# Convolution and routed feed-forward: ids turned later, turns pinned behind results, rows listed for scatter sooner

## The chip, the cores and the metric

The kernel runs on one core of one Trainium2 chip. The metric is the device time of one execution in microseconds. Before the change the median of three runs is 1252.04 us (1251.1 to 1256.04). The engines are named as in the profile: PE is TensorE's matmul, PEld its weight load, DVE is VectorE, ACT is ScalarE, POOL is GpSimd, SP is SyncE, which here only issues transfers.

## The reference, cut to what matters

```
# 1. a causal convolution, 7 taps, 8 heads with their own softmaxed weights
w   = softmax(weight)                       # 8 x 7
x1  = sum over k of w[h, k] * x_pad[b, s + k, h, :]        # x: 8 x 3584 x 192
# 2. each of the 28672 rows goes to one of 8 experts
logits = x1 @ w_gate + modality_bias[modality_id]          # 192 -> 8
e      = argmax(logits);  gate = softmax(logits)[e]
out    = gate * (relu(x1 @ w1[e]) @ w2[e])  # 192 -> 1024 -> 192, in float32
```

## The kernel before, in words

**Routing.** The sequence is cut into blocks of 120 rows. 19 groups of 4, 8 or 16 tiles (`QUADS_OF_GROUP`, in quads of 4 tiles) pass through the same parts (`body`, lines 671 to 705, and `finish`, 655 to 669). A group is convolved on PE into PSUM, one product for a head or a pair of heads, and ACT (some heads: DVE) copies the result into a row buffer `y` (lines 427 to 462; L446, L448 and L460, L462). `turn` (L478) transposes 32 x 32 squares of y on DVE, a quad at a time, so that PE can multiply them by the gate weights (L496, L512). DVE turns the logits back (L503, L518), adds the bias `bt` of the row's modality (L504, L520; POOL makes it at L473 and L476), and `choose` finds the expert. `place` counts the rows of each expert with products of the one-hot choice and keeps a running `carry`; from these come the row numbers `idx` (L620) in a scratch table of routed rows. Groups from 6 on are `tiled`: all 128 partitions are used for the small arrays, and `move` and `take` bring the numbers back into place. `send` lists one scatter a tile: POOL writes 120 rows of y to their places in the scratch table (L347, an indirect DMA).

There are four y buffers, and a group of 16 tiles takes two. So the copies of group g overwrite rows that group g - 2 scatters.

**Experts.** When a chunk of groups has been routed (`GROUPS_OF_CHUNK`), `table` works out on DVE which experts have enough rows for a slot of fixed size. A slot loads its expert's weights (SP, L895 to L900), splits them and its rows into a high and a low part (L110, L112, L980, L982), and runs in steps. A step is 20 products of the first layer (`first`, L995), the relu on ACT (hh, L998), its low part on DVE (hl, L999), and 16 products of the second layer for the step two before (`second`, L1015, L1019). Every four steps `put` weighs the result (lowp on ACT, o on DVE, L1033) and POOL writes two tiles of out (L1037). There are 456 steps.

**Order.** `run` writes steps and routing parts into each other: after each step it advances the routing generator until the parts reach `due(step)`. The first four groups and 59 parts more come before step 0. Scatters and out writes aren't issued where they are written but put into the list `waiting` (`in_turn`); out writes go to its front. After each step `release` takes one out of it, or two when more than `MANY` wait, and makes it wait for the hl of that step (`behind_step`). Before group g is convolved, `release_rows_of(g - 2)` empties the list of that group's rows at once. How fast scatters are listed is set in `all_groups`: the ends of group g - 1 (its place, numbers and scatters: 22 of them) are spread over the parts of group g (25 or 29). ACT's instructions within the steps keep the order in which they are written. The other engines' lists are ordered by a planner, which takes what it holds to be ready; `tc.issue_after(ins)` puts what is inside it behind `ins` on the same engine and adds nothing else. `turn_squares`, the transposes of a slot's rows, are already behind `state["o"]`, which is the last hl or o that has been written.

**Modality ids.** Those of groups 0 to 5 come first, by POOL's DMAs. Those of the later groups are loaded by SP (`load_later`, L307) into the second weight buffer `raw1[1]`, and `make_mods`, called in front of group 5, casts them (L252), transposes them (L254), and hands them to all later `bias_of`. `make_tiled` (L229) builds the tables of the tiled groups on POOL; its last two operations (L245, L246) are DVE's.

Of the kernel before, what the change touches and what calls it, by code (L numbers as in the profile page):

```python
# [9 lines left out]
F32 = mybir.dt.float32  # L10
# [4 lines left out]
ALU = mybir.AluOpType  # L15
AX = mybir.AxisListType
PSUM = bass.MemoryType.PSUM

P = 128
MB = 120  # L20
# [16 lines left out]
AHEAD = 59  # L37
SPLIT = 46
T = 256
MANY = 4  # L40
GROUPS_OF_CHUNK = (4, 3, 2, 2, 2, 2, 2, 2, 0, 0)
SLOTS_OF_CHUNK = (3, 2, 3, 4, 3, 4, 4, 3, 4)
PASSES_OF_SLOT = (2, 4, 4, 4, 4, 4, 4, 4, 2, 1)
# [8 lines left out]
def conv_then_routed_ffn(ctx, tc, x, weight, modality, w_gate, mod_bias, w1, w2, out):  # L52
    nc = tc.nc
    NB, S, D = x.shape
    H, K = weight.shape
    E, _, FF = w1.shape
# [9 lines left out]
    OVER = 2  # L66
    Q = 32
    NK = D // Q
    W = D + OVER
# [9 lines left out]
    const = ctx.enter_context(tc.tile_pool(name="const", bufs=1))  # L79
# [11 lines left out]
    turns, state = {}, {}  # L91

    def ring(pool, n, shape, dtype, name, tag=None):

        tag = tag or name
        k = turns[tag] = turns.get(tag, -1) + 1
        return pool.tile(shape, dtype, name=name, tag=f"{tag}_{k % n}", bufs=1)
# [10 lines left out]
    def split(hi, lo, raw, behind=None):  # L108
        with tc.issue_after(behind[0]) if behind else nullcontext():
            nc.scalar.copy(out=hi, in_=raw)  # L110
        with tc.issue_after(behind[1]) if behind else nullcontext():
            return nc.vector.tensor_tensor(out=lo, in0=raw, in1=f(hi), op=ALU.subtract).ins  # L112


    def make_marks():
# [27 lines left out]
                      in_=weight.rearrange("h k -> (h k)").partition_broadcast(K * DIAG))  # L143
# [12 lines left out]
    def warm(n):  # L156
# [9 lines left out]
        out=tri, in_=ones, compare_op=ALU.is_gt, fill=0.0, base=0,  # L166
# [62 lines left out]
    def make_tiled():  # L229

        wide = const.tile([P, NK, Q], F32, name="wg_wide")
        nc.gpsimd.memset(wide, 0.0)
        same = const.tile([P, P // Q, Q], F32, name="same")
        part = const.tile([P, P // Q], F32, name="part")
        nc.gpsimd.memset(part, 0.0)
        for q in range(P // Q):
            rows = slice(q * Q, (q + 1) * Q)
            nc.gpsimd.memset(part[rows, q:q + 1], 1.0)
            nc.gpsimd.tensor_copy(out=wide[rows, :, q * E:(q + 1) * E], in_=wg[rows])
            nc.gpsimd.tensor_copy(out=same[rows], in_=ident[rows, rows].unsqueeze(1).broadcast_to([Q, P // Q, Q]))  # L240
        ramps = const.tile([P, P // Q, E], F32, name="ramps")
        nc.gpsimd.iota(ramps, pattern=[[0, P // Q], [-1, E]], base=E, channel_multiplier=0,
                       allow_small_or_imprecise_dtypes=True)
        real = const.tile([P, 1], F32, name="real")
        nc.vector.tensor_reduce(out=real, in_=same[:, 0, 0:MB % Q], axis=AX.X, op=ALU.add)  # L245
        nc.vector.tensor_scalar(out=ramps[:, MB // Q, :], in0=ramps[:, MB // Q, :], scalar1=real, scalar2=None, op0=ALU.mult)  # L246
        return wide, same, part, ramps

    def make_mods():

        low = raw1[1][:, 1, 0:LOTS * P].rearrange("p (b s) -> p b s", s=Q)
        nc.vector.tensor_copy(out=low, in_=later.rearrange("p l (q s two) -> p (l q) s two", s=Q, two=2)[:, :, ::-1, 0])  # L252
        mods = const.tile([P, LOTS, P // Q, Q], F32, name="mods")
        nc.vector.transpose(out=mods.rearrange("p l q r -> p (l q r)"), in_=low.rearrange("p b s -> p (b s)"))  # L254
        return mods
# [44 lines left out]
    def load_later():  # L300
        nc.vector.memset(later[:, LOTS - 1, :].bitcast(F32), 0.0)
        for c in range(P // Q):
            for lot in range(LOTS):
                n = min(8, NG - TILED - 8 * lot)
                b, sb = c % 2 * 4, EARLY + 16 * lot + c // 2
                at = 2 * (b * S + sb * MB - CUT + MB - P)
                nc.sync.dma_start(out=later[c * Q:c * Q + 4 * n, lot], in_=bass.AP(words.tensor, words.offset + at, [  # L307
                    [4 * MB, n], [2 * S, 4], [1, 2 * P]]))
# [4 lines left out]
    later = raw1[1][:, 0, 0:LOTS * 2 * P].bitcast(I32).rearrange("p (l w) -> p l w", l=LOTS)  # L313
# [15 lines left out]
    def release(n=1):  # L329
        while waiting and n:  # L330
            op, _ = waiting.pop(0)
            n -= op() is not None
# [36 lines left out]
    class Group:  # L369
# [108 lines left out]
        def turn(self, q):  # L478

            t0 = self.b0 + 4 * q % NB  # L480
            if not self.tiled:
                dst = ring(gp, 2, [P, NK, 4, Q], F32, "turned")
                self.quad_turned.append(dst)
            else:
                if q == 0:
                    self.turned = xp.tile([P, NK, NT, Q], F32, name="gx", tag=self.place_x)
                dst = self.turned[:, :, 4 * q:4 * q + 4]
            nc.vector.transpose(out=dst.rearrange("p k t c -> p t k c"),
                                in_=self.ys[4 * q // NB][:, t0:t0 + 4, OVER:W].rearrange("p t (k c) -> p t k c", c=Q))

        def gate_tiled(self):

# [154 lines left out]
    def parts_of(g):  # L647

        return H + 5 + 3 * QUADS_OF_GROUP[g] + (QUADS_OF_GROUP[g + 1] if WHOLE_X <= g + 1 < NG else 0)

    def ends_of(g):

        return 4 * QUADS_OF_GROUP[g] + (6 if g >= TILED else 1)

    def finish(gr, at_once):
        gr.place()
        yield
        if gr.tiled:
            yield
            yield  # L660
            gr.move()
            yield
            yield
            gr.take()
            yield
        for t in range(0, gr.tiles, at_once):
            gr.send(t, t + at_once)
            yield
        in_turn(lambda: state.update(groups=state["groups"] + 1), gr.g)
# [37 lines left out]
    early, wide = [], []  # L707

    def load_early(g):
        early.append(Group(g, chunk_of[g]))  # L710
        for q in range(early[-1].quads):
            early[-1].load(q)

    def all_groups():

        for g in range(CLEARED, sum(len(p) for p in PACKS)):
            load_early(g)
        with tc.issue_after(state["x"]):
            ins = nc.sync.dma_start(out=scr[DUMMY:DUMMY + TW, :].rearrange("(j p) w -> p j w", p=P),
                                    in_=filler.unsqueeze(1).broadcast_to([P, TW // P, W])).ins  # L720
        tc.add_to_no_dep_group("rows0", ins)
        scatters.append((0, ins.name))
        load_later()
        cur, ends = early[0], iter(())
        for g in range(NG):
            if g == TILED - 1:
                wide.append(make_mods())
            if g == WHOLE_X - 2:
                split(band_hi, band_lo, band)
            after = (early[g + 1:g + 2] or [Group(g + 1, chunk_of[g + 1])])[0] if g + 1 < NG else None  # L730
            done = 0
            for i, _ in enumerate(body(cur, after)):
                yield
                if g < FIRST:
                    if 1 <= i < H:
                        next(ends, None)
                        if i == H - 1:
                            for _ in ends:
                                pass
                elif g == KEPT:  # L740
                    next(ends, None)
                else:
                    while done * (parts_of(g) - 4) < ends_of(g - 1) * i:
                        next(ends, None)
                        done += 1
            for _ in ends:
                pass
            ends = finish(cur, 4 if g < FIRST else 1)
            if g + 1 in (FIRST, NG):
                for _ in range(WAIT):  # L750
                    yield
                for _ in ends:
                    yield
            cur = after
# [291 lines left out]
    plan, tokens, slots, g = [], 0, 0, 0  # L1046
# [18 lines left out]
    start_row, step, low = make_modality()  # L1065
# [5 lines left out]
    with tc.issue_after(state["low"]):  # L1071
        filler = make_filler()
    state.update(carry=carry, groups=0, placed=0, brought=0, parts=0)
    work = all_groups()

    def advance():
        next(work, None)
        state["parts"] += 1
# [18 lines left out]
    for c in range(1, last):  # L1097
        steps += plan[c - 1][1] * steps_of(c - 1)
        g = sum(GROUPS_OF_CHUNK[:c + 1])
# [47 lines left out]
    def run(i0, i1):  # L1147

        lagging, count = [], 0
        for i in range(i0, i1):  # L1150
# [3 lines left out]
            for step in range(steps):  # L1154
# [10 lines left out]
                while i0 == 0 and state["parts"] < due(count):  # L1165
                    advance()
                release(1 + (len(waiting) > MANY))
                if chunk < last and state["placed"] >= sum(GROUPS_OF_CHUNK[:chunk + 2]) and \
# [85 lines left out]
```

## Time and profile before

| | |
|---|---|
| median of the runs | 1252.04 us |
| the profiled execution | 1254.28 us |
| its span, first to last instruction | 1252.2 us |
| mean granted TensorE clock | 0.986 |
| PE busy | 1204.0 us, 96% |
| DVE busy | 930.4 us, 74% |
| ACT busy | 693.2 us, 55% |
| POOL busy | 514.7 us, 41% |

The span is one profiled execution; what a run takes outside it is the 2.1 us between the second and the third line. An engine's busy time is a sum over the whole span; where the engine waits, and for whom, is in the timelines and in the view of waits. An idle time stands in brackets behind an instruction, with the instruction that released it.

### The profile page before, as it was taken

The numbers are of one execution on the slowest core, as the hardware profiler recorded it, in microseconds if no ns is written. First come the engines' busy times: TensorE is split into PE (matmuls) and PEld (weight loads), VectorE is DVE, ScalarE is ACT, GpSimd is POOL, SyncE is SP. The second block draws the span as 40 slices with busy tenths as digits, with TensorE's granted clock in tenths as the row PEclk, the third lists the DMA queues.
The fourth block names the chain that finished last, engine by engine and source line by source line (L and its number), as shares of the span: only waits on it lengthen the run. The fifth ranks groups of instructions, "written<-read, shape, count | busy, mean of one in ns | idle before, by whom it ended". The sixth has DMA issues, their size and how long they took to land. (4 is left out here: it accounts for less than half of the span.)

```text
span 1252.2 us, 28508 instructions
## 1 busy us (share of the span) xinstructions
PE 1204.0 (96%) x9507; PEld 1180.0 (94%) x9507; DVE 930.4 (74%) x2427; ACT 693.2 (55%) x1545; POOL 514.7 (41%) x568
## 2 busy tenths in 40 slices
PE   7889999999999999999999999999999999999996
PEld 6789999999999899998999999999999999999995
DVE  5787887677777777777776786876866766787894
ACT  2365555554655455555555555655555555566783
POOL 6746645534435245262624525335243222222121
PEclk8899999999999999999999999999999999999998
DMA  6787645335534353343543525433254343944271
GB/s 165 215 212 216 138 116 137 82 98 149 142 58 127 83 125 97 67 116 89 150 89 73 123 59 130 101 63 75 76 120 89 83 92 87 274 101 109 43 187 42
DMA packets 307587, 143.85 MB, mean 115 GB/s; under 512 B 221899, under 2 KB 294103, under 8 KB 307430
## 3 DMA queue, kind: packets, MB, share of 16 engines
q1 hardware_dynamic: 283894, 97.57, 35.5%
q0 software_dynamic: 22560, 44.34, 11.3%
q8 instruction: 76, 1.25, 0.4%
q14 instruction: 81, 0.66, 0.2%
q10 hardware_dynamic: 976, 0.03, 0.0%
HBM read 116.13 MB, written 51.81 MB: 134 GB/s over the span
## 5 line engine op out<-in xcount | busy, mean ns | idle before, releaser
L1015 PE MATMUL po<-w2b,hh 128*128 128x384 f32 x1824 | 558.6, 357 | 3.9 <-DVE o L1033 3.9
L995 PE MATMUL hps<-sxh,w1b 128*128 128x256 f32 x1824 | 485.1, 288 | 16.4 <-DVE hl L999 14.8
L999 DVE SCALAR_TENSOR_TENSOR hl<-hps,hh 128x512 fp32r<-128x512 f32 x456 | 313.2, 688 | 217.1 <-ACT hh L998 213.0
L1037 POOL DMA_INDIRECT out_dram<-o,tags x228 | 231.1, 1013 | 554.7 <-DVE o L1033 334.8
L998 ACT ACTIVATE hh<-hps 128x512 fp32r<-128x512 f32 x456 | 273.0, 599 | 320.8 <-PE hps L995 317.1
L1019 PE MATMUL po<-w2b,hl 128*128 128x192 f32 x1824 | 444.2, 254 | 0.0
L995 PEld LDWEIGHTS hps<-sxh,w1b 128*128 128x128 f32 x1824 | 344.6, 189 | 27.8 <-DVE hl L999 24.7
L995 PE MATMUL hps<-sxs,w1b 128*128 128x256 f32 x1824 | 363.4, 281 | 0.3 <-DVE sxs L982 0.2
L1015 PEld LDWEIGHTS po<-w2b,hh 128*128 128x128 f32 x1824 | 345.0, 189 | 5.4 <-DVE o L1033 5.1
L1019 PEld LDWEIGHTS po<-w2b,hl 128*128 128x128 f32 x1824 | 347.5, 191 | 0.0
L347 POOL DMA_INDIRECT routed_rows<-y,idx x240 | 252.4, 1052 | 166.5 <-DVE hl L999 74.2
L995 PEld LDWEIGHTS hps<-sxs,w1b 128*128 128x128 f32 x1824 | 279.7, 189 | 0.7 <-DVE sxs L982 0.4
L995 PE MATMUL hps<-sxl,w1b 128*128 128x256 f32 x912 | 256.7, 282 | 0.7 <-DVE sxl L982 0.7
L995 PEld LDWEIGHTS hps<-sxl,w1b 128*128 128x128 f32 x912 | 173.1, 190 | 0.9 <-DVE sxl L982 0.9
L112 DVE TENSOR_TENSOR w1b<-raw,w1b 128x512 fp32r<-128x512 f32 x152 | 101.7, 678 | 25.1 <-ACT w1b L110 24.9
L1031 ACT ACTIVATE lowp<-po,tags 128x192 f32<-128x192 f32 x228 | 83.8, 419 | 30.9 <-PE po L1015 30.9
L112 DVE TENSOR_TENSOR w2b<-raw,w2b 128x384 fp32r<-128x384 f32 x152 | 80.9, 542 | 19.9 <-ACT w2b L110 19.6
L110 ACT CAST w1b<-raw 128x512 fp32r<-128x512 f32 x152 | 92.8, 621 | 1.9 <-DMA raw<-in_moe_w_dram 0.7
L1033 DVE SCALAR_TENSOR_TENSOR o<-po,tags,lowp 128x192 f32<-128x192 f32 x228 | 84.8, 411 | 2.2 <-ACT lowp L1031 2.2
L980 ACT CAST sxs<-tp 64x128 fp32r<-64x128 f32 x224 | 66.7, 298 | 31.5 <-DVE tp L954 28.8
L110 ACT CAST w2b<-raw 128x384 fp32r<-128x384 f32 x152 | 76.0, 512 | 1.4
L982 DVE TENSOR_TENSOR sxs<-tp,sxs 64x128 fp32r<-64x128 f32 x224 | 64.3, 287 | 9.1
(191 smaller groups left out, 846.8 us busy)
## 6 DMA issues: line engine op xcount, KB each, us to landing
raw<-in_moe_w_dram SPq DMA_DIRECT2D x38, 768.0 KB
raw<-in_moe_w_dram SPq DMA_DIRECT2D x38, 512.0 KB
raw<-in_moe_w_dram SPq DMA_DIRECT2D x76, 256.0 KB
near<-routed_rows SPq DMA_DIRECT2D x208, 64.0 KB
xr<-in_x_dram SPq DMA_DIRECT2D x32, 384.0 KB
x<-in_x_dram SPq DMA_DIRECT2D x26, 384.0 KB
routed_rows<-filler SPq DMA_DIRECT2D x9, 776.0 KB
far<-routed_rows SPq DMA_DIRECT2D x208, 32.0 KB
```

The lines of the kernel that those rows point to most:

```text
L110: nc.scalar.copy(out=hi, in_=raw)
L112: return nc.vector.tensor_tensor(out=lo, in0=raw, in1=f(hi), op=ALU.subtract).ins
L347: state["scatter"] = nc.gpsimd.indirect_dma_start(out=scr, out_offset=bass.IndirectOffsetOnAxis(ap=idx, axis=0), in_=src, in_offset=None,).ins
L980: nc.scalar.copy(out=hi, in_=raw)
L995: nc.tensor.matmul(hps[:, u, :], wa[:, c, fs], mv[z], start=n == 0, stop=n == len(terms) - 1)
L998: state["hh"] = nc.scalar.activation(out=hh, in_=hps, func=AF.Relu).ins
L999: hl_ins = nc.vector.scalar_tensor_tensor(out=hl, in0=hps, scalar=0.0, in1=f(hh), op0=ALU.max, op1=ALU.subtract)
L1015: nc.tensor.matmul(po, hh[:, u, js], wb[:, c, :], start=c == 0, stop=c == NF - 1, skip_group_check=True)
L1019: nc.tensor.matmul(po[:, 0:D], hl[:, u, js], wb[:, c, 0:D], start=False, stop=False, skip_group_check=True)
L1031: nc.scalar.activation(out=lowp, in_=po[:, D:2 * D], func=AF.Copy, scale=gate)
L1033: turn_behind(nc.vector.scalar_tensor_tensor(out=o, in0=po[:, 0:D], scalar=gate, in1=lowp, op0=ALU.mult, op1=ALU.add))
L1037: st = nc.gpsimd.indirect_dma_start(out=out, out_offset=bass.IndirectOffsetOnAxis(ap=at, axis=0), in_=o, in_offset=None, bounds_check=N - ...
```

## The change

Four edits. `MANY` falls from 4 to 3, so two are released after a step when more than three wait. `make_tiled` no longer ends with the two operations on `real` and `ramps`; they move into `make_mods`, and both they and the cast of the later ids (with the transpose that needs it) go behind `state["idx"]`, which at that place of the text is the row numbers of group 3. The transposes of `turn` go behind the last hl or o, as soon as there has been one. And the ends of a group are spread over nine parts fewer than the next group has, where it was four fewer.

```
-MANY = 4
+MANY = 3
...
+        return wide, same, part, ramps
+
+    def make_mods():
+
+        _, same, _, ramps = wide
         real = const.tile([P, 1], F32, name="real")
-        nc.vector.tensor_reduce(out=real, in_=same[:, 0, 0:MB % Q], axis=AX.X, op=ALU.add)
+        with tc.issue_after(state["idx"]):
+            nc.vector.tensor_reduce(out=real, in_=same[:, 0, 0:MB % Q], axis=AX.X, op=ALU.add)
         nc.vector.tensor_scalar(out=ramps[:, MB // Q, :], in0=ramps[:, MB // Q, :], scalar1=real, scalar2=None, op0=ALU.mult)
-        return wide, same, part, ramps
-
-    def make_mods():
-
         low = raw1[1][:, 1, 0:LOTS * P].rearrange("p (b s) -> p b s", s=Q)
-        nc.vector.tensor_copy(out=low, in_=later.rearrange("p l (q s two) -> p (l q) s two", s=Q, two=2)[:, :, ::-1, 0])
+        with tc.issue_after(state["idx"]):
+            nc.vector.tensor_copy(out=low, in_=later.rearrange("p l (q s two) -> p (l q) s two", s=Q, two=2)[:, :, ::-1, 0])
...
-            nc.vector.transpose(out=dst.rearrange("p k t c -> p t k c"),
-                                in_=self.ys[4 * q // NB][:, t0:t0 + 4, OVER:W].rearrange("p t (k c) -> p t k c", c=Q))
+            with tc.issue_after(state["o"]) if "o" in state else nullcontext():
+                nc.vector.transpose(out=dst.rearrange("p k t c -> p t k c"),
+                                    in_=self.ys[4 * q // NB][:, t0:t0 + 4, OVER:W].rearrange("p t (k c) -> p t k c", c=Q))
...
-                    while done * (parts_of(g) - 4) < ends_of(g - 1) * i:
+                    while done * (parts_of(g) - 9) < ends_of(g - 1) * i:
```

## Rows read from the trace of the kernel before

**Rows 1.** The page's first part: busy us, share of the span, instructions.
```profile
PE 1204.0 (96%) x9507; PEld 1180.0 (94%) x9507; DVE 930.4 (74%) x2427; ACT 693.2 (55%) x1545; POOL 514.7 (41%) x568
```

**Rows 2.** Windows: length, busy us of each engine, granted clock, DMA share, GB/s.
```profile
250.00:275.00 25.00, 22.72 (x158) 22.17 (x157) 18.16 (x51) 14.22 (x34) 10.66 (x10) 0.93 0.48 120
...
400.00:425.00 25.00, 21.95 (x156) 21.32 (x156) 17.68 (x39) 14.02 (x31) 9.30 (x9) 0.93 0.71 163
...
550.00:575.00 25.00, 22.85 (x160) 22.29 (x158) 18.03 (x52) 14.04 (x33) 11.01 (x10) 0.93 0.48 123
...
950.00:975.00 25.00, 25.00 (x196) 25.00 (x196) 17.17 (x42) 14.76 (x32) 7.50 (x8) 1.00 0.33 60
```

**Rows 3.** Waits of PE, whole span: total us, times, longest us.
```profile
PE hps L995 <- DVE hl L999: 14.8, 14, 3.0
PE gt L512 <- DVE turned L488: 5.6, 1, 5.6
PE po L1015 <- DVE o L1033: 3.9, 5, 1.7
```

**Rows 4.** Waits of ACT, whole span, in front of the copy into y.
```profile
ACT y L446 <- DMA out_dram<-o,tags: 25.2, 6, 5.2
```

**Rows 5.** Timeline of ACT, 262 to 276: start, us, instruction, idle before.
```profile
266.48 0.77 ACT L446 COPY y<-cv 120x192 f32<-120x192 f32 x3 [4.76 <-DMA out_dram<-o,tags]
```

**Rows 6.** Timeline of POOL, 225 to 300: the last scatter before that copy.
```profile
261.33 0.99 POOL L347 DMA_INDIRECT routed_rows<-y,idx  x1 [0.35 <-DVE hl L999]
```

**Rows 7.** Waits of PE in 250:300, 325:360, 400:430, 550:600, 625:665 and 700:750.
```profile
PE hps L995 <- DVE hl L999: 3.2, 3, 2.3
...
PE hps L995 <- DVE hl L999: 1.6, 1, 1.6
...
PE hps L995 <- DVE hl L999: 3.0, 1, 3.0
...
PE hps L995 <- DVE hl L999: 3.0, 3, 2.1
...
PE hps L995 <- DVE hl L999: 1.9, 1, 1.9
...
PE hps L995 <- DVE hl L999: 1.0, 2, 0.8
```

**Rows 8.** Timeline of DVE: turns before the steps, and in them.
```profile
56.52 3.55 DVE L488 STREAM_TRANSPOSE gx<-y 128x768 f32<-128x768 f32 x4
...
287.63 0.96 DVE L488 STREAM_TRANSPOSE gx<-y 128x768 f32<-128x768 f32 x1
288.53 0.64 DVE L999 SCALAR_TENSOR_TENSOR hl<-hps,hh 128x512 fp32r<-128x512 f32 x1
```

**Rows 9.** Timeline of DVE in the head: the later ids, the tiled logits.
```profile
18.16 0.31 DVE L252 CAST raw<-raw 128x256 f32<-128x256 int32 x1 [6.21 <-DMA raw<-in_moe_modality_id_dram]
...
62.08 0.29 DVE L504 TENSOR_TENSOR lg<-lt,bt 128x128 f32<-128x128 f32 x1
```

**Rows 10.** Timeline of PE in the head: convolution, gate, first step.
```profile
11.65 2.27 PE L457 MATMUL cv<-x,band 128*120 128x96 f32 x18
19.50 2.90 PE L512 MATMUL gt<-turned,wg_whole 128*128 128x128 f32 x12 [5.58 <-DVE turned L488]
...
62.67 0.51 PE L995 MATMUL hps<-sxh,w1b 128*128 128x256 f32 x2
```

**Rows 11.** Timeline of POOL in the head: tables, bias, scatters.
```profile
19.10 0.18 POOL L242 IOTA ramps<- 128x32 f32 x1
20.02 0.83 POOL L473 TENSOR_TENSOR bt<-mods,step 128x128 f32<-128x128 f32 x2 [0.74 <-DVE mods L254]
...
27.96 1.11 POOL L347 DMA_INDIRECT routed_rows<-y,idx  x1 [6.28 <-DVE oh L557]
...
53.34 1.12 POOL L347 DMA_INDIRECT routed_rows<-y,idx  x1 [0.30 <-issue]
...
57.76 0.99 POOL L347 DMA_INDIRECT routed_rows<-y,idx  x1 [0.30 <-issue]
```

More of the change, by code (lines that the diff above doesn't have):

```diff
@@ L243, in make_tiled @@
                        allow_small_or_imprecise_dtypes=True)
-        real = const.tile([P, 1], F32, name="real")
-        nc.vector.tensor_reduce(out=real, in_=same[:, 0, 0:MB % Q], axis=AX.X, op=ALU.add)
-        nc.vector.tensor_scalar(out=ramps[:, MB // Q, :], in0=ramps[:, MB // Q, :], scalar1=real, scalar2=None, op0=ALU.mult)
         return wide, same, part, ramps
     def make_mods():
+        _, same, _, ramps = wide
+        real = const.tile([P, 1], F32, name="real")
+        with tc.issue_after(state["idx"]):
+            nc.vector.tensor_reduce(out=real, in_=same[:, 0, 0:MB % Q], axis=AX.X, op=ALU.add)
+        nc.vector.tensor_scalar(out=ramps[:, MB // Q, :], in0=ramps[:, MB // Q, :], scalar1=real, scalar2=None, op0=ALU.mult)
         low = raw1[1][:, 1, 0:LOTS * P].rearrange("p (b s) -> p b s", s=Q)
-        nc.vector.tensor_copy(out=low, in_=later.rearrange("p l (q s two) -> p (l q) s two", s=Q, two=2)[:, :, ::-1, 0])
+        with tc.issue_after(state["idx"]):
+            nc.vector.tensor_copy(out=low, in_=later.rearrange("p l (q s two) -> p (l q) s two", s=Q, two=2)[:, :, ::-1, 0])
         mods = const.tile([P, LOTS, P // Q, Q], F32, name="mods")
```

## The prediction

> **What bounds the kernel now.** I read the windows first, then the waits, then the timelines around the waits. TensorE (PE) is busy 1204.0 of 1252.2 us [rows 1], and in the late stretch 950 to 975 it is busy for all of it at full clock [rows 2]. So a step costs what PE needs for it, and this change touches no matmul. What can move is the 48 us in which PE stands, and the clock that is lost behind a pause: in the stretches at 250, 400 and 550 PE is busy 21.95 to 22.85 of 25 us and the granted clock averages 0.93, so it has fallen to its lower level, 1.2 GHz, for part of them [rows 2]. At 0.93 for 25 us, 0.07 x 25 = 1.75 us of full-speed work is lost in each.
>
> The waits of PE sort into three kinds. Most is PE waiting for hl, 14.8 us in 14 waits, then 5.6 us in one wait for a turned row, then 3.9 us for o [rows 3].
>
> First kind: y that can't be overwritten. ACT copies the convolution into y, and ACT runs in written order, so what stands behind that copy (the relu hh of a step) stands too. These copies waited 25.2 us in six waits [rows 4]; the one at 266.48 waited 4.76 us for a DMA [rows 5]. The last scatter from the rows that it overwrites was issued at 261.33 and off POOL at 262.32 [rows 6], so it took 4.2 us more to land. The view names a write of out as the releaser; no operand of the copy has to do with out, and a wait for several signals is put down to the one that came last, so I read it as the scatter. PE then waits for hl: longest waits 2.3, 1.6, 3.0, 2.1, 1.9 and 0.8 us, one for each of the six copies, 11.7 us [rows 7].
>
> Second kind: turns of a group in a bunch. At 287.63 DVE runs a turn of 0.96 us, and hl starts right behind it at 288.53 [rows 8]. The third and fourth turn of that group are written several steps apart, but DVE's list has them in a row. What is left of PE's waits for hl, 14.8 - 11.7 = 3.1 us, and the 3.9 us for o are of this kind: 7.0 us.
>
> Third kind: the head. DVE's copy of the later modality ids stands 6.21 us for its DMA until 18.16 [rows 9], and the first turned rows stand behind it. PE, done with two groups' convolutions at 13.92, waits 5.58 us for them until 19.50 [rows 10].
>
> **The change part by part.**
>
> Rows five parts sooner, and MANY 3. No instruction is added: the same 240 scatters, listed and released earlier. I counted through the rules of `release`, `release_rows_of` and `ends` step by step. Before, 3 to 5 scatters of a group are still waiting when the group two later starts, and are all released in the step that also issues that group's convolution (groups 7 to 16). After, none of them is: the last one is released 5 or 6 steps ahead for groups 9 to 16 and 2 steps ahead for groups 7 and 8; group 6 stays as it is (8 left in place of 9). From 62.67 [rows 10] to the end 456 steps take 2.6 us each, so five steps are 13 us, against 4.2 us to land. The six waits should go, and with them three of the clock dips: 11.7 + 3 x 1.75 = 16.9 us. What is late next there is DVE: the row-number chain of the group before starts in the same steps. I take 14 of the 16.9 us; bounds 0 (landing is set by something else) and 16.9. Two releases a step from a queue of four fill POOL earlier, not more; POOL is busy for 514.7 of 1252.2 us [rows 1], so it costs nothing while the out writes stay in front, which `in_turn` sees to.
>
> Turned rows behind a step's results. 13 groups have four turns each; 12 of them (48 turns of 0.96 us) are issued within the steps. Pinned behind the last hl or o, no turn can be drawn forward, and the bunches fall apart into one turn in two to four steps. Gain at most 7.0 us, all waits of the second kind. Queued behind a pinned turn on DVE are the other splits and transposes of that step; who waits for the turn itself is the gate product on PE. The choice of an expert is written 5 to 8 steps behind the last turn, and the row numbers come after that, so a turn that is 0.96 us late has room. Below nothing: PE runs in order, and if a gate product is put too early in its list, PE stands for the turn; the nearest rows are 5.58 us in the head [rows 10] and, per group, one step of 2.6 us. I take 3.5 us gained, half of the upper bound, since the turns of the first group in the steps are written in successive steps and stay dense.
>
> Modality ids behind the first row numbers. Removed from in front of the first turn: the copy with its 6.21 us, and the transpose and the two small operations on `real` and `ramps`, all moved behind the fourth group's row numbers, where they cost DVE at most 4 x 0.31 [rows 9], about 1 us. DVE was free for the first turn at 18.16 - 6.21 = 11.95; the gate product behind that turn then stands behind the convolutions, at 13.92 in place of 19.50, and at full clock, since the stretch without PE work goes. From there to the first scatter the rows take 27.96 - 19.50 = 8.5 us [rows 10, 11], part of it at the lower clock. POOL is the floor: its preparation of the tiled tables ends at 19.10 + 0.18 [rows 11], so the first scatter can't be much ahead of 19.7: at most 8.2 us sooner than 27.96. From there POOL paces the head: 20 scatters (4, 4, 8 and 4 tiles of the first four groups) start from 27.96 to 53.34 [rows 11], and the first slot's rows are read when the 20th has landed. The two bias pairs on POOL (`bt`, 0.83 us for the first two operations [rows 11], about 1.7 us for all four) need the ids and move from in front of the scatters to among them; they delay the scatters behind them by 1.7 us, or not the first slot's at all if they come behind the 20th. The ids lie in the weights' second buffer, which is asked for only after the first slot's rows are. I take 6 us sooner for the first step; bounds 8.2 us, and 1 us later (DVE's moved 1 us with nothing won). PE is the bound of all that follows, so the lead stays to the end.
>
> A rule of the skill against it: the scatter at 57.76 took 0.99 us under four turns that ran on DVE from 56.52 on, 3.55 us long [rows 8, 11], as long as others. The Trainium skill, SBUF — State Buffer, section "SBUF: two separate sides", says that while a VectorE operation holds the port pair that it shares with GpSimd, GpSimd can't write the descriptors of its DMAs until that operation ends. The pin makes turn and scatter start together, both being released by hl. By the rule a scatter would land up to 0.96 us later, which hurts only groups 7 and 8 with their two steps: 1.9 us more of ACT's waits, of which PE lost 11.7 / 25.2, so 0.9 us, and the sum would be 1230. By the row it costs nothing, and I go by the row.
>
> **Sum.** 14 + 3.5 + 6 = 23.5 us. The profiled execution took 1254.28 us, 2.1 outside its span; less 23.5 that is 1230.8. The median of the runs shown is 1252.04, and from that it is 1228.5. I say 1229.
>
> **Rivals.**
>
> A. The head's lead is lost (0.20). If POOL's list has the bias pairs behind all 32 early scatters (20 take 25.4 us [rows 11] and 12 more another 16, with what lies between 43), they run at 19.7 + 43 = about 63, and the logits of the first tiled group, at 62.08 before [rows 9], come no sooner; if the first step's operations stand behind them, the head gains nothing. For it: POOL is full then. Against it: nothing makes step 0 need them. Time: 1252 - 17.5 = 1234.5.
>
> B. Listing sooner doesn't free y (0.13). The landing of 4.2 us [rows 5, 6] may be set by the loads of the next slot's rows, which fill the DMA engines then, or the wait may be for the out write that is named. Then the six waits stay, and only head and turns change; with both at half, 1252 - 5 = 1247. Against it: 13 us is far more than 4.2.
>
> C. Slower (0.09): PE stands for late turns. One mechanism: the gate products sit in PE's list where the planner thinks the last turn ends; on the chip hl is late, the turn behind it too, and PE stands up to one step, 2.6 us, in each of 12 groups: 31 us, against 20 us won in the two other parts (14 + 6): 1252 + 11 = 1263. It decides from 20 / 12 = 1.7 us a group. For it: PE has already waited 5.58 us for one turn. Against it: a group's turns have steps of room before anything needs them.
>
> **How the numbers follow.** Forecast 0.58, A 0.20, B 0.13, C 0.09. The forecast's own range is 1219 (everything at its upper bound, 16.9 + 7.0 + 8.2 = 32.1 less) to 1240. With A inside and part of B, the range is 1218 to 1250. A measurement of this kernel tells apart about 0.5%, 6 us. Forecast and A are faster by more; B is within it: faster 0.78, same 0.13, slower 0.09.
>
> **What would show it.** ACT's waits for a DMA in front of L446 gone (25.2 us before), PE's waits for hl under 6 us, the windows that had 0.93 at 1.00. No two turns (L488) in a row on DVE after the first step. First scatter near 20, first product L995 near 56. I am wrong if PE's idle time in the steps moves to another wait, above all `gt` for `gx`, or if the first scatter is early and the first L995 isn't.

## The result, and the profile after

The changed kernel takes 1236.0 us (median of four, 1234.91 to 1236.26); the kernel before took 1251.57 us (median of four) on the same chip. The ratio is 0.9868 [0.9842, 0.9895], 15.6 us less. 23.5 us less were forecast, and 1229. On another chip, beside experiments told below, the changed kernel took 1234.18 us where the kernel before took 1254.54: 0.9847 [0.9824, 0.9871]. So it is faster, by 16 to 20 us, and by less than forecast.

The page's first part: DVE, ACT and POOL have the same work to within 3 us, and PE is busy 9.9 us less than in [rows 1].

```profile
PE 1194.1 (97%) x9507; PEld 1171.9 (95%) x9507; DVE 933.4 (76%) x2427; ACT 692.1 (56%) x1545; POOL 515.5 (42%) x568
```

The windows of [rows 2], after the change:

```profile
250.00:275.00 25.00, 25.00 (x188) 24.77 (x188) 22.22 (x66) 17.02 (x41) 6.37 (x6) 1.00 0.44 103
400.00:425.00 25.00, 24.97 (x187) 24.66 (x187) 21.44 (x71) 14.70 (x36) 5.33 (x5) 1.00 0.44 95
550.00:575.00 25.00, 25.00 (x190) 24.93 (x188) 21.29 (x77) 14.57 (x38) 7.55 (x7) 1.00 0.42 109
950.00:975.00 25.00, 25.00 (x197) 25.00 (x196) 18.74 (x59) 14.15 (x31) 4.90 (x5) 1.00 0.30 52
```

PE stood for 2 to 3 us in each of the first three and ran at 0.93; now it is busy throughout at 1.00. The waits of PE over the whole span, as in [rows 3] (us in total, times, longest):

```profile
PE cv L460 <- DMA x<-in_x_dram: 9.5, 1, 9.5
PE hps L999 <- DVE hl L1003: 5.2, 14, 0.5
PE gt L516 <- DVE den L564: 3.1, 1, 3.1
PE po L1019 <- DVE o L1037: 1.7, 2, 1.0
PE moved L628 <- DVE spread L612: 1.5, 1, 1.5
```

The waits for hl fell from 14.8 to 5.2 us and none is longer than 0.5, those for o from 3.9 to 1.7. But there is a new one at the top: 9.5 us for a load of x. (Lines stand three or four further down than before: L995 is L999, L446 is L449.) Of ACT's waits for a DMA in front of a copy into y, the 25.2 us of [rows 4] are gone as a whole; what is left of this kind (5.4 us in one wait before) is

```profile
ACT y L463 <- DMA routed_rows<-y,idx: 9.6, 2, 6.7
```

at 107.3 and 118.6 us, the copies that overwrite the rows of group 6, of which, by the prediction's count of the lists, eight scatters are still forced out. DVE's turns between 278 and 299 us, which were in a bunch [rows 8], now stand 3 to 8 us apart:

```profile
279.36 0.95 DVE L492 STREAM_TRANSPOSE gx<-y 128x768 f32<-128x768 f32 x1
...
287.53 0.97 DVE L492 STREAM_TRANSPOSE gx<-y 128x768 f32<-128x768 f32 x1
...
290.65 0.97 DVE L492 STREAM_TRANSPOSE gx<-y 128x768 f32<-128x768 f32 x1
...
297.64 0.97 DVE L492 STREAM_TRANSPOSE gx<-y 128x768 f32<-128x768 f32 x1
```

From the first hl to the last one (456 of them) took 1171.35 us before and takes 1151.80: the steps gained 19.5 us. The spans of the two profiled executions differ by 18.2 us (1252.2 and 1234.0), so the head (all that comes before the first step), from which 6 us were forecast, gave nothing: the first hl comes 1.2 us later. The head's beginning went as forecast. On POOL, for [rows 11]: the first scatter at 20.77 (27.96 before), the 20th at 46.07 (53.34), the bias pairs behind it.

```profile
20.77 1.11 POOL L350 DMA_INDIRECT routed_rows<-y,idx  x1 [0.73 <-ACT y L463]
...
46.07 1.32 POOL L350 DMA_INDIRECT routed_rows<-y,idx  x1 [0.30 <-issue]
47.40 0.15 POOL L569 IOTA y<- 120x4 int32 x1
47.63 0.82 POOL L476 TENSOR_TENSOR bt<-mods,step 128x128 f32<-128x128 f32 x2
48.41 1.32 POOL L479 TENSOR_TENSOR bt<-bt,both 128x128 f32<-128x128 f32 x2
```

On PE, for [rows 10]: the first gate product at 14.08 (19.50 before), and then, at the end of the head, the first product of the first layer at 63.68, where it was at 62.67. In front of it PE stands 9.48 us.

```profile
14.08 1.08 PE L516 MATMUL gt<-turned,wg_whole 128*128 128x128 f32 x8
...
57.10 2.88 PE L460 MATMUL cv<-x,band 128*120 128x192 f32 x8 [9.48 <-DMA x<-in_x_dram]
...
63.68 0.51 PE L999 MATMUL hps<-sxh,w1b 128*128 128x256 f32 x2
```

The reason is seen on SP. After the change (first fence) three loads of x go out behind the first slot's rows, before it (second fence) two:

```profile
49.80 0.96 SPq L934 DMA_DIRECT2D raw<-routed_rows  x2
50.95 0.37 SPq L934 DMA_DIRECT2D tags<-routed_rows  x1
51.38 1.74 SPq L416 DMA_DIRECT2D x<-in_x_dram  x3
```

```profile
56.29 0.96 SPq L930 DMA_DIRECT2D raw<-routed_rows  x2
57.44 0.37 SPq L930 DMA_DIRECT2D tags<-routed_rows  x1
57.87 1.13 SPq L413 DMA_DIRECT2D x<-in_x_dram  x2
```

The slot's rows wait for 20 scatters to land, and SP issues in the order of its list. The load that has come behind them is the second x of group 7: it waits for the scatters with them, and PE, whose list has group 7's convolution ahead of the first step, waits for that load.

### The profile page after: what moved, and what is told of

It reads as the page before. It is cut to its first block, busy times and chain, and to the rows that moved or that the text cites. A ratio compares the mean times of both kernels' runs of the same rounds, so it can differ in the third digit from the quotient of the medians.

```text
span 1234.0 us, 28502 instructions
## 1 busy us (share of the span) xinstructions
PE 1194.1 (97%) x9507; PEld 1171.9 (95%) x9507; DVE 933.4 (76%) x2427; ACT 692.1 (56%) x1545; POOL 515.5 (42%) x568
## 4 chain that ended last, share of the span: by engine, by line
PE 73%; DVE 6%; issue 4%; DMA 3%; ACT 2%; POOL 1%; SPq 1%; DVEq 0%; POOLq 0%
PE hps L999 35%; PE po L1019 22%; PE po L1023 10%; PE cv L444 3%; DVE hl L1003 1%; DMA raw<-in_moe_w_dram 1%; PE gt L500 1%; DMA xr<-in_x_dram 1%; PE cv L460 1%; DVE w2b L112 1%; ACT lowp L1035 1%; DVE w1b L112 1%; POOL out_dram L1041 1%; ACT hh L1002 1%; SPq L934 1%
## 5 line engine op out<-in xcount | busy, mean ns | idle before, releaser
L999 PE MATMUL hps<-sxh,w1b 128*128 128x256 f32 x1824 | 482.6, 287 | 6.3 <-DVE hl L1003 5.2
L1041 POOL DMA_INDIRECT out_dram<-o,tags x228 | 236.7, 1038 | 556.1 <-DVE o L1037 318.2
L999 PE MATMUL hps<-sxs,w1b 128*128 128x256 f32 x1824 | 363.1, 281 | 0.3 <-DVE sxs L986 0.2
L999 PEld LDWEIGHTS hps<-sxh,w1b 128*128 128x128 f32 x1824 | 343.5, 188 | 15.8 <-DVE hl L1003 12.6
L350 POOL DMA_INDIRECT routed_rows<-y,idx x240 | 246.8, 1028 | 146.7 <-issue 69.9
L999 PEld LDWEIGHTS hps<-sxs,w1b 128*128 128x128 f32 x1824 | 278.6, 188 | 0.7 <-DVE sxs L986 0.4
L999 PE MATMUL hps<-sxl,w1b 128*128 128x256 f32 x912 | 255.8, 281 | 0.3 <-DVE sxl L986 0.3
L999 PEld LDWEIGHTS hps<-sxl,w1b 128*128 128x128 f32 x912 | 172.4, 189 | 0.5 <-DVE sxl L986 0.4
L984 ACT CAST sxh<-tp 128x256 fp32r<-128x256 f32 x112 | 45.8, 409 | 50.1 <-DVE tp L956 50.1
```

What stands on the lines that cost most here:

```text
L350: state["scatter"] = nc.gpsimd.indirect_dma_start(out=scr, out_offset=bass.IndirectOffsetOnAxis(ap=idx, axis=0), in_=src, in_offset=None,).ins
L999: nc.tensor.matmul(hps[:, u, :], wa[:, c, fs], mv[z], start=n == 0, stop=n == len(terms) - 1)
L1041: st = nc.gpsimd.indirect_dma_start(out=out, out_offset=bass.IndirectOffsetOnAxis(ap=at, axis=0), in_=o, in_offset=None, bounds_check=N - ...
```

## The experiments

Two theories were named ahead of them. Theory 1: the steps gain because scatters have landed before their y is overwritten, and the head's lead is lost to the order of loads on SP. Theory 2: the steps gain because turns are pinned. Five runs of each kernel at the least, each in turn with the kernel before on the same chip; a ratio is to that.

### One edit at a time, on the kernel before

On this chip the kernel before took 1254.15 us (median of 23).

**Nine parts fewer alone.**

```
-                    while done * (parts_of(g) - 4) < ends_of(g - 1) * i:
+                    while done * (parts_of(g) - 9) < ends_of(g - 1) * i:
```

> The kernel before with one edit: ends spread over nine parts fewer. Theory 1 (the gain in the steps comes from scatters that have landed before y is overwritten): ACT's waits for a DMA in front of the copy into y (25.2 us in six) fall to 3 us or less, PE's waits for hl from 14.8 to about 5 us, no granted clock of 0.93 after 100 us, and 12 to 17 us less, about 1237. Theory 2 (the gain comes from the pinned turns): the waits of ACT may go, but PE stays late behind the turns; at most 4 us less.

1233.7 us, 0.9842 [0.9818, 0.9865]: 20 us less, as much as all four edits give and more than the 12 to 17 expected. From the first to the last hl took 1151.5 us, as with all four, and the windows of [rows 2] are at full clock without any pin:

```profile
250.00:275.00 25.00, 25.00 (x188) 24.80 (x187) 21.80 (x65) 16.89 (x40) 9.64 (x10) 1.00 0.47 112
400.00:425.00 25.00, 24.96 (x188) 24.66 (x187) 21.50 (x70) 14.61 (x36) 5.32 (x5) 1.00 0.45 93
550.00:575.00 25.00, 24.68 (x185) 24.36 (x184) 22.83 (x78) 14.08 (x37) 6.53 (x7) 1.00 0.41 108
```

Waits of PE (from the second row of the view on), then waits of ACT for a DMA, whole span:

```profile
PE po L1015 <- DVE o L1033: 4.4, 6, 1.7
PE cv L457 <- ACT y L460: 3.8, 2, 3.3
PE hps L995 <- DVE hl L999: 2.1, 6, 0.5
```

```profile
ACT y L460 <- DMA routed_rows<-y,idx: 5.3, 1, 5.3
ACT y L446 <- DMA routed_rows<-y,idx: 3.7, 4, 1.1
```

The waits of ACT that the view put down to a write of out are gone, though every write of out is still there: they were waits for scatters. With them went 12.7 of the 14.8 us that PE waited for hl. The trace of the kernel before says the same by its semaphore updates, which tell when a transfer lands: those of the scatter issued at 261.33 [rows 6] come from 264.98 to 266.33, and the copy of [rows 5] starts at 266.48, while those of the write of out issued at 263.95 run on to 267.38. In four more of the six waits the copy starts as close behind the last scatter (0.14 to 0.18 us), with a write of out still landing.

**MANY 3 alone.**

```
-MANY = 4
+MANY = 3
```

> The kernel before with MANY 3 alone. By the count of the lists the last rows leave one step sooner; for the copies of groups 13, 14, 17 and 18 none is left to be forced out (two steps of room), for groups 9 to 12, 15 and 16 three or four still are. Theory 1: the waits at groups 13 and 17 go (PE 3.0 + 0.8 us and one clock dip of 1.75), those at 11, 12, 15 and 16 stay: 4 to 6 us less, about 1247. Theory 2: no change.

1244.0 us, 0.9917 [0.9901, 0.9932]: 10 us less, where 4 to 6 were expected. Two of the six waits, at groups 13 and 17, fell to 1.5 and 1.3 us, and four stayed (ACT's waits for a DMA):

```profile
ACT y L446 <- DMA out_dram<-o,tags: 14.8, 4, 4.5
ACT y L460 <- DMA routed_rows<-y,idx: 12.0, 3, 4.7
```

By the rules of release none is left forced out for groups 11, 12, 15 and 16 and 3 to 4 for the six others, so a part of the waits goes and a part stays. PE's waits for hl fell to 8.5 us, and the way from the first hl to the last one is 6.6 us shorter in the profile; what the rest of the 10 is, isn't shown. This edit changes only the release, while the nine parts also bring the row numbers forward; both take away the same waits. This edit and the nine parts pay for the same thing, and as the run with both shows (below), they don't add up.

**Turns pinned alone.**

```
-            nc.vector.transpose(out=dst.rearrange("p k t c -> p t k c"),
+            with tc.issue_after(state["o"]) if "o" in state else nullcontext():
+                nc.vector.transpose(out=dst.rearrange("p k t c -> p t k c"),
```

> The kernel before with the turns pinned alone. Theory 1: ACT's six waits stay at 25 us; the short waits of PE behind turns (7.0 us) shrink by a third: 0 to 4 us less, about 1250. Theory 2: 10 us less or more, about 1240.

1251.99 us (12 runs), 0.9988 [0.9972, 1.0004]: no difference that can be told, though 3.5 us less would still lie at the edge of the interval. (The profile is of the second fastest of the 12 runs.) The turns are apart as they are after the whole change, and PE waits less for o (3.9 before) and as long for hl (14.8 before):

```profile
PE hps L996 <- DVE hl L1000: 15.6, 18, 2.3
...
PE po L1016 <- DVE o L1034: 1.0, 1, 1.0
```

Theory 2 falls.

**Ids moved alone** (`real`, `ramps` and the cast of the later ids, as in the change):

```
+        return wide, same, part, ramps
+
+    def make_mods():
+
+        _, same, _, ramps = wide
         real = const.tile([P, 1], F32, name="real")
+        with tc.issue_after(state["idx"]):
...
-        return wide, same, part, ramps
-
-    def make_mods():
-
...
+        with tc.issue_after(state["idx"]):
```

> The kernel before with the ids moved alone. Theory 1 (the lead of the head is lost again because one load of x for group 7 now stands behind the loads of the first slot's rows in SP's list): first scatter near 21, PE waits about 9.5 us for x near 57, first product of the first layer at 63 to 64 in place of 62.67, and the time is the same within 2 us. Rival: the lead is lost to the later edits (scatter listing), then this kernel alone keeps it and is 6 to 7 us faster, about 1245.

1251.49 us (12 runs), 0.9980 [0.9967, 0.9994], about 2.5 us less, a little more than the expected 2. The first scatter is at 20.69 us, 7.3 sooner, the first product of the first layer at 61.62, 1.05 sooner (63 to 64 was expected), and the wait for x is there with this edit alone:

```profile
55.62 2.88 PE L460 MATMUL cv<-x,band 128*120 128x192 f32 x8 [9.27 <-DMA x<-in_x_dram]
...
61.62 0.50 PE L998 MATMUL hps<-sxh,w1b 128*128 128x256 f32 x2
```

### The load moved, and the two listing edits together

On this chip the kernel before took 1254.54 us (median of 9). The changed kernel once more:

> The changed kernel once more, unaltered, so that the two next stand beside it on one chip. On the first chip it was at 0.987 of the kernel before, on a chip where all is some 4% slower its neighbours without the pin, without the moved ids and with another load order were at 1.004, 1.012 and 1.005. Theory 1 (steps gain 19.5 us from the earlier scatters, head loses about 1 us to an x load behind the first slot's row loads): about 0.986 of the kernel before on a chip where that takes some 1252 us, first product of the first layer at 63 to 64 us, about 9 us of waiting for x ahead of it. If the chip is one of the slow ones: 1.00 to 1.01, no x wait, first product after 72 us.

1234.18 us, 0.9847 [0.9824, 0.9871]; first product at 62.27, a wait of 9.3 us for x. It is 1.4 us earlier there than in the first profile of the same kernel, so one profile's head is good to some 1.4 us.

**The load moved.** In the changed kernel, the first slot is brought only behind group 7's second x load on SP.

```
+            state["x_of", self.g, q] = ld.ins
...
-        bring(lots.index((i, 0)))
+            make(0)
+        else:
+            bring(lots.index((i, 0)))
...
+            if i == 0 and not state["brought"] and ("x_of", FIRST + 3, 1) in state:
+                with tc.issue_after(state["x_of", FIRST + 3, 1]):
+                    bring(0)
```

> The changed kernel with group 7's second x load handed to SyncE ahead of the first slot's row loads. Theory 1: the 9.5 us wait for x ahead of group 7's convolution goes, and of the 7 us by which the first scatter is earlier 4 to 7 us reach the first product of the first layer (57 to 60 us instead of 63.7); 1229 to 1232 us beside 1236 of the changed kernel on the same chip. Rival (the head is held by its chain of groups anyway, and the x wait only stands where another wait would be): the first product stays at 62 us or later and the time within 2 us of the changed kernel's.

1228.88 us (1227.54 to 1230.86), 0.9798 [0.9776, 0.9821]: 5.3 us under the changed kernel on the same chip; the runs of the two don't overlap (1227.54 to 1230.86 and 1233.86 to 1237.51), and it is 25.7 under the kernel before. SP's list, then PE's:

```profile
39.52 1.42 SPq L416 DMA_DIRECT2D x<-in_x_dram  x2
50.60 0.98 SPq L935 DMA_DIRECT2D raw<-routed_rows  x2
51.77 0.37 SPq L935 DMA_DIRECT2D tags<-routed_rows  x1
52.20 0.58 SPq L416 DMA_DIRECT2D x<-in_x_dram  x1
```

```profile
49.28 1.57 PE L461 MATMUL cv<-x,band 128*120 128x192 f32 x8 [2.69 <-ACT y L464]
...
57.41 0.53 PE L1000 MATMUL hps<-sxh,w1b 128*128 128x256 f32 x2
```

The two x loads go out 11 us ahead of the slot's rows, the wait for x is gone, and the first product comes 4.9 us sooner than in the changed kernel beside it (57.41, 62.27). The steps take 1152.2 us, and 1151.5 without the move. So on this chip the cause of the lost head is shown.

**Both listing edits** on the kernel before, ids and turns as they were (the two edits above together):

> The kernel before with both listing edits (nine parts fewer and two a step over three waiting), ids and turns left as they were. Theory 1: the steps take as long as in the changed kernel (1152 us from the first to the last hl) and the head as long as before (first product near 62.5 us), so 1232 to 1236 us, level with the changed kernel or 1 to 3 us under it, and no more than nine parts fewer alone gave (1233.7 us on its chip). Theory 2 (the pinned turns are worth 3 us or more): 3 us or more over the changed kernel.

1236.8 us (1233.8 to 1238.57), 0.9850 [0.9826, 0.9874]: level with nine parts fewer alone and with all four edits, if at the upper end of what was expected. The profile is of the slowest of the five runs, with the first product at 64.69, where 62.5 was expected; the steps take 1153.6 us. Two of PE's waits:

```profile
PE po L1015 <- DVE o L1033: 3.9, 5, 1.7
PE hps L995 <- DVE hl L999: 3.2, 8, 0.8
```

Against the changed kernel (hl 5.2 us in 14 waits, o 1.7 in 2) this is what the pin does: 2.2 us less waiting for o, 2.0 us more for hl, in waits of 0.5 us at most. (The moved ids, the other difference, left the waits for o at 3.9 us and those for hl at 15.3 when they were moved alone.)

### On two chips where all is slower

Five more runs fell on two chips on which the kernel before took 1307.11 us (median of 23) and 1304.84 (median of 17), some 4% more than elsewhere. The expectations were written for chips like the first.

**The changed kernel with the load moved**, as above:

> The changed kernel, with the second load of x for group 7 pinned ahead of the loads of the first slot's rows in SP's list; all else as it was. Theory 1: PE's wait of 9.5 us for x goes, the first product of the first layer comes at 55 to 58 in place of 63.7, and the lead stays to the end: 6 to 8 us less than the changed kernel, about 1229. Rival (POOL's 32 scatters or the landing of the first slot's rows bound the head anyway): PE waits as long for the rows or the logits, first product at 61 or later, less than 3 us gained.

1314.56 us, 1.0054 [1.0031, 1.0077]. The first product comes at 72.08. The two loads that were moved go out 1 us ahead of the slot's rows here, not 11:

```profile
51.95 0.04 SPq L416 DMA_DIRECT2D x<-in_x_dram  x2
53.04 0.98 SPq L935 DMA_DIRECT2D raw<-routed_rows  x2
```

**The changed kernel with the ids where they were** (the reverse of "ids moved"):

> The changed kernel without the move of the ids. Theory 1: the move was worth nothing or 1 us lost, so 1234 to 1237, and the head as before (first product at 62.7). Rival (the move won its 6 us and something else lost them): 1241 or more.

1325.01 us, 1.0124 [1.0084, 1.0164].

**Both listing edits on the kernel before:**

> The kernel before with both list edits (nine parts fewer, MANY 3). Theory 1: all of the gain in the steps but the pin's share is here, 13 to 18 us less, 1234 to 1239. Theory 2: at most 6 us less.

1326.25 us, 1.0131 [1.0089, 1.0172].

**The changed kernel with the turns not pinned** (the reverse of "turns pinned"):

> The changed kernel without the pin of the turns. Theory 1: turns come in bunches again, PE's short waits for hl and o rise by 2 to 4 us: 1237 to 1240. Theory 2 (the pin made the gain): 1246 or more. If the pin costs something: under 1235.

1311.12 us, 1.0038 [1.0014, 1.0061]. The x loads are not moved here, and yet PE has no wait for x; the first product comes at 72.87. So on these chips no run shows a gain from moving the loads (the two kernels differ in the pin too).

**The load moved, turns not pinned, and `MANY = 4`**, on the second of the two chips:

```
-MANY = 3
+MANY = 4
...
-            with tc.issue_after(state["o"]) if "o" in state else nullcontext():
```

> Two of the four edits (ids turned later, nine parts fewer) and group 7's second x load ahead of the first slot's row loads; the turns not pinned, two rows a step only over four waiting, as in the kernel before. Theory 1 (pinned turns and MANY 3 are worth nothing once rows are listed sooner): 1227 to 1231 us on a chip where the kernel before takes 1254, level with all four edits and the load moved (1228.9), first product of the first layer near 57.4 us, about 1152 us from the first to the last hl. Theory 2 (pinned turns or MANY 3 are worth 2 us or more): 1231 to 1235 us with the first product as early.

1311.47 us, 1.0044 [1.0027, 1.0060]. It was to say whether pin and MANY 3 are worth 2 us beside the moved load on a chip like the first; for such a chip that stays open. Here it is level with the kernel that has both (1.0054).

So on these two chips none is faster than the kernel before, and the listing edits, 18 us less on one chip, are 19 us more on another (1326.25 against 1307.11). The traces show what is different in kind. In the run with both listing edits PE's waits begin with

```profile
PE po L1015 <- DVE o L1033: 26.1, 22, 2.0
PE gt L496 <- issue: 15.2, 26, 1.1
```

and in its timeline gate products come one at a time, 0.72 us apart, with nothing in the trace that they wait for:

```profile
170.79 0.27 PE L496 MATMUL gt<-gx,wg_wide 128*32 128x128 f32 x1 [0.32 <-issue]
171.52 0.28 PE L496 MATMUL gt<-gx,wg_wide 128*32 128x128 f32 x1 [0.47 <-issue]
172.24 0.27 PE L496 MATMUL gt<-gx,wg_wide 128*32 128x128 f32 x1 [0.44 <-issue]
```

DVE has 62.2 us of such idle time in front of hl there, in 57 waits; the same kernel on the faster chip has 3.1 us in two, and PE none in front of gt. PE is busy 1231.2 of 1325.0 us, so it stands 94 us, where the same kernel stood 39. What holds the instructions back no view names. Of the kernel before and of the changed kernel there is no profile from these chips, so where the 19 us come from, and whether the changed kernel itself is slower there, is open; the three that differ from it by one edit are 0.4 to 1.2% slower than the kernel before.

One thing is told there: the kernel with turns not pinned and the one with both listing edits differ in the ids alone, and the moved ids are worth 15 us (1311.12 against 1326.25), of which 11.3 are in the head (first product at 72.87 against 84.13). The other kernels agree: with moved ids the first product is at 72.08 and 71.90 us, without them at 84.93.

## Why the prediction was right, and where it was off

**Rows listed sooner: right, under-sized.** Forecast 14 us, upper bound 16.9. Nine parts fewer alone shortened the way from the first to the last hl by 19.8 us. PE's idle time on that way fell from 23.3 to 8.8 us (summed over its records): 12.7 less for hl, 2.1 less in one wait for `spread`, 0.5 more for o. The three dips of the clock at 271, 421 and 572 us went too, each 3.4 us at 1.2 GHz in place of 2.4, so 1.7 us each, 5.1 together; the dip at 93 got longer and cost 1.7. 14.5 + 5.1 - 1.7 = 17.9 of the 19.8. The other 1.9 I can't place. So both terms of the 16.9 were right within 1 us where they were looked for (5.1 for the dips, 12.7 for hl with 11.7 in the six waits), but 16.9 was no upper bound, and taking 14 of it was too careful.

**Turned rows pinned: not shown to be worth anything.** Forecast 3.5 us; alone the pin gave 2.2 by the medians, with an interval from 3.5 less to 0.5 more, and beside the listing edits nothing that can be told. Of the 3.1 us of waiting for hl that I put down to bunches, 1.0 went with the listing and 2.1 are left without any pin; with the pin it is 5.2, so these waits weren't the pin's to take. The 3.9 us for o were the turns' and fell to between 1.0 and 1.7, but beside the listing edits the pin gave as much back in small waits for hl. Rival C didn't come: PE never stood for a turn in the steps.

**Modality ids: the failing step is "I take 6 us sooner for the first step".** Forecast 6 us; in the first profile of the changed kernel the first product came 1.0 us later, in the second 0.4 sooner, and with the ids moved alone 1.05 sooner and 2.5 us less in time. Up to POOL all was as forecast: first scatter at 20.77 (19.7 at the earliest), 20th 7.3 us sooner, bias pairs behind it at no cost. What I left out was SP's list. I followed the scatters to the slot's rows and took the first step to start with them; but PE does group 7's convolution first, and the load that this needs was put behind the slot's rows, in a list that stands until the 20th scatter has landed. With the load ahead of them 5.3 us are there (62.67 in the kernel before to 57.41 in the profiles, and 1234.18 to 1228.88 in time), near the 6. The step behind it held: 4.9 us won ahead of the first step (62.27 to 57.41, same chip) were 5.3 us at the end, so a lead that reaches the first step does stay. So the term was right for a head in which the loads keep their order, on a chip like these.

**The sum was helped by luck.** 23.5 us were forecast, 15.6 and 20.4 came, and 1236.0 lies within the range of 1218 to 1250. The listing gave 5.8 us more than its 14, and that covered a good part of the 9.5 us that the pin and the ids were to give and, by the profiles of the changed kernel, didn't. That the kernel with the load moved takes 25.7 us less, near the forecast, is again with a larger term for the listing and none that can be told for the pin. (The lower end of the forecast's own range, everything at its upper bound, is 1220, not 1219.)

**The rivals.** A has the time (1234.5), not the cause: it wanted the bias pairs behind 32 scatters, they came behind 20, and nobody waited. B is excluded: with nine parts fewer alone ACT's 25.2 us are gone. The rule of the Trainium skill that I weighed (SBUF — State Buffer, "SBUF: two separate sides") was to cost 0.9 us in ACT's waits for scatters of groups 7 and 8. The section lets a VectorE operation lock GpSimd out only in a 2-port mode or, with two SBUF inputs, against a GpSimd operation that reads; the prediction took a turn for such an operation without a reason. No run here shows a cost of this kind: the waits for scatters that grew, 9.6 us in front of L463, are as long without any pin (4.2 and 5.4 us in the same two places with both listing edits alone).

**What I asked of the profile.** Waits of ACT gone, hl under 6 us, 1.00 in the windows, no two turns in a row (ten such pairs in the steps before, none after), first scatter near 20: all as said. First L995 near 56: not so, and "if the first scatter is early and the first L995 isn't" was the condition under which I would be wrong.

## What to carry to other kernels

Where a wait for a buffer repeats in every group, free the buffer well ahead by its list, and look for one edit that does it: on top of that one, the others added nothing to the steps here. Before a lead is credited to the end, follow it on every queue that stands between, and ask what a blocking transfer (rows that wait for scatters) has behind it in the issuing engine's list and who waits for that. A release that a view names can be another: the waits named for a write of out went with the scatters.

## What the runs showed of the hardware

Two of the chips run the kernel before 4% slower than the others (1305 and 1307 us against 1252 to 1255). Its granted clock averages 0.971 to 0.982 in the runs there and 0.983 to 0.992 on the others; by an estimate from these two ranges that is 1 of the 4%. The profiles of the other versions there have idle time of PE, DVE and ACT that no view explains, and the order of the versions is another one. A gain of 1.5% that was measured on one chip isn't a gain on each.

A scatter of 120 rows that left POOL at 262.32 had its last semaphore update at 266.33: it took 4.0 us to land, 5.0 from its issue.
